# A spectral-mixing and gated MLP kernel: the sequence DFT in a three-fold split, with the odd half turned on ScalarE and GpSimd

## The chip, the cores and the metric

One core of a Trainium2 chip runs the whole kernel. The metric is the device time of the core in microseconds (us). A profile is one execution; "span" is its length, about 2 us below the timed value.

Engine names: PE is TensorE's matmul, PEld its weight load, DVE VectorE, ACT ScalarE, POOL GpSimd, SP SyncE. A fp32 matmul is two records in the trace. A "step" is one turn of the main loop; there are 376. A "record pitch" is the time from one PE record's start to the next.

## The reference

```python
def _attn_ref(x):                    # x: (8, 3008, 256) float32
    X = np.fft.fft(x, axis=1)        # over the sequence
    X = np.fft.fft(X, axis=2)        # over the channels
    return X.real.astype(np.float32)

def _moe_ref(x, w_in, w_out):        # (24064, 256), (256, 2048), (2048, 256)
    h = x @ w_in
    g = h * np.cos(h)
    return (g @ w_out).astype(np.float32)
# reference: the second of the first, with x reshaped to (24064, 256)
```

## The kernel before

The channel DFT is folded into `w_in` once (eight pairs of 512-column matmuls, giving `Wc` and `Ws`). The sequence DFT of a batch gives rings `Rr` and `Ir`, from which the main loop takes 256 columns a tile. Each step makes h on PE, its gate on ACT and DVE, four sums on POOL, and the second matmul with sums of w_out blocks (`WT`). The DFT of the next batch is spread over the loop: POOL folds rows `n` and `SEQ-n`, then PE multiplies folded rows by cosine and sine tables.

```python
# six row groups per batch of 128 (some partly used); even half and odd half
NH = (190, 189); NE = 377; NO = 376
def dft_parts(ri, kodd, par):
    mats = MC[ri, kodd]; nh = NH[kodd]
    if not par:                                   # four matmuls of 189/190 columns
        for t, m in enumerate((C0, Y, C2, Y)):
            yield m, t // 2 * nh, mats[:, t * nh : (t + 1) * nh]
        return
    c = 4 * nh
    if kodd: parts = ((D1, 0, NO), (X1, 0, NO), (M1, 0, NO))     # 3 x 376 columns
    else:    parts = ((6, 0, NK), (M1, NK, NE - NK), (X1, 0, NE))
    ...
# start: CC and half of w_in are loaded first, then batch 0's rows, then the rest
load_w1(0); L_first = load_x(0)
for g in gathers(0): gather_x(0, L_first, g)
...
# ... (cut)
def sum_weights(i):                               # WT by four POOL sums a pair of blocks
    gtt(W[2], b12, b22, ALU.add); gtt(W[1], b11, W[2], ALU.subtract)
    gtt(W[0], b12, b11, ALU.subtract); gtt(W[3], W[1], b21, ALU.add)
# batch 0's folds on DVE before the loop; those of later batches on POOL, spread over 36 steps
```

Of the kernel before, what the change touches and what calls it, by code (L numbers as in the profile page):

```python
# [26 lines left out]
NE = 377  # L27
NO = 376
NK = 189
NH = (190, 189)  # L30
MW = (4 * NH[0] + 2 * NE, 4 * NH[1] + 3 * NO)
C0, D1, C2, Y, M1, X1 = range(6)
# [4 lines left out]
def _row_of(m):  # L37

    p = np.arange(128)
    return (4 * p, 247 - 2 * p, 4 * p + 2, 504 + 2 * p, 505 + 2 * p, 249 + 2 * p)[m]  # L40


def _dft_consts():

    every = np.ones(128, bool)
    first, last = np.arange(128) % 2 == 0, np.arange(128) % 2 == 1
    used = {C0: 126, D1: 124, C2: 126, Y: 125, M1: 124, X1: 128}
    parts = []
    for kodd in range(2):
        if kodd:  # L50
            half = np.arange(NH[1])
            odd = [(m, every, np.arange(NO)) for m in (D1, X1, M1)]
        else:
            half = np.concatenate([np.arange(0, NH[0], 2), np.arange(1, NH[0], 2)])
            two = [np.arange(q, NE, 2) for q in range(2)]
            odd = [(D1, every, k) for k in two] + [(X1, every, np.concatenate(two))]
        even = [(C0, every, half), (Y, first, half), (C2, every, half), (Y, last, half)]
        for ri in range(2):
            fn = np.cos if ri == 0 else np.sin
            for m, keep, kk in even + odd:  # L60
                s = _row_of(m)
                k = 2 * kk + kodd
                v = fn(2.0 * np.pi * ((s[:, None] * k[None, :]) % SEQ) / SEQ)
                v[used[m] :] = 0.0
                v[s == 0] *= 0.5
                v[s == RUN] *= 0.5 if ri == kodd else 0.0
                v[~keep] = 0.0
                parts.append(v)
    return np.concatenate(parts, axis=1).astype(np.float32)
# [15 lines left out]
def _pick_consts():  # L85

    m = np.zeros((128, 56), np.float32)
    m[np.arange(128), np.arange(128) % 32] = 1.0
    q = np.arange(32)
    c = 32 + q % 16 // 2  # L90
    m[q, c] = 1.0
    m[q, c + 8] = np.where(q // 16 == q % 2, 1.0, -1.0)
    m[q, c + 16] = -1.0
    return m


def _row_consts():

    cols = [_row_of(D1), HALF + _row_of(D1)]
    for base in (HALF, SEQ):  # L100
        cols += [base - _row_of(m) for m in (C2, M1, X1)]
    cols += [SEQ - _row_of(m) for m in (C0, D1)]
    return np.clip(np.stack(cols, axis=1), 0, SEQ - 1).astype(np.uint32)
# [3 lines left out]
def kernel(  # L107
# [13 lines left out]
    MC_dr = nc.inline_tensor(_dft_consts(), name="dft_mats")  # L121
    CC_dr = nc.inline_tensor(_chan_consts(), name="chan_mats")
    PK_dr = nc.inline_tensor(_pick_consts(), name="pick_mats")
    IX_dr = nc.inline_tensor(_row_consts(), name="row_table")
# [15 lines left out]
    def xrows(b, row, step, n, rows=6):  # L140

        return bass.AP(
            tensor=xt,
            offset=x.offset + (b * SEQ + row) * ND,
            ap=[[step * ND, n], [1, rows * ND]],
        )
# [3 lines left out]
    ix = cpool.tile([128, 10], U32, tag="ix")  # L150
    nc.sync.dma_start(out=ix, in_=IX_dr.ap())

    def gather_x(b, L, g):

        j, part, n = g
        pin(
            nc.gpsimd.indirect_dma_start(
                out=L[j][:, part[0] * ND : part[1] * ND],
                out_offset=None,
                in_=xflat,  # L160
                in_offset=bass.IndirectOffsetOnAxis(ap=ix[:, n : n + 1], axis=0),
                element_offset=b * SEQ * ND,
            )
        )

    def spin(**kw):
        pin(nc.sync.dma_start(**kw))

    def gathers(b):

        yield 0, (1, 2), 0
        yield 3, (1, 2), 1
        for j, n in ((2, 2), (1, 5)):
            if j == 2 or b < NB - 1:
                yield j, (3, 6), n
            else:
                yield j, (3, 4), n
                yield j, (5, 6), 8
                yield j, (4, 5), 9
            yield j, (1, 3), n + 1  # L180
            yield j, (0, 1), n + 2

    def load_x(b):
        L = [
            spool.tile([128, 6 * ND], FP, tag=f"xl{j}", bufs=1, name=f"xl{j}")
            for j in range(4)
        ]
        for j, row in ((0, 0), (3, HALF)):
            spin(
                out=L[j].rearrange("p (m d) -> p m d", d=ND)[:, C0 : C2 + 1 : 2],  # L190
                in_=bass.AP(
                    tensor=xt,
                    offset=x.offset + (b * SEQ + row) * ND,
                    ap=[[4 * ND, 128], [2 * ND, 2], [1, ND]],
                ),
            )
            spin(out=L[j][:, Y * ND : X1 * ND], in_=xrows(b, row + 504, 2, 128, 2))
            spin(out=L[j][:, X1 * ND :], in_=xrows(b, row + 249, 2, 128, 1))
        return L

    def load_d(b, L, j):
        if b < NB - 1 or j == 2:
            row = SEQ if j == 1 else HALF
            spin(out=L[j][:, 4 * ND : 5 * ND], in_=xrows(b, row - 247, 2, 128, 1))



    CC = cpool.tile([128, 512], FP, tag="CC")
    spin(out=CC, in_=CC_dr.ap())
    w1 = {}  # L210

    def load_w1(half):
        for h in range(2):
            if h == 0:
                t = spool.tile([128, GW], FP, tag="G", bufs=3, name="w1")[:, 0:1024]
            else:
                t = spool.tile([128, 1024], FP, tag="ot", bufs=2, name="w1")
            w1[h, half] = t
            spin(
                out=w1[h, half],  # L220
                in_=moe_w_in[h * 128 : (h + 1) * 128, half * 1024 : (half + 1) * 1024],
            )

    load_w1(0)
    L_first = load_x(0)
    for g in gathers(0):
        gather_x(0, L_first, g)
    load_d(0, L_first, 2)
    load_w1(1)
    load_d(0, L_first, 1)  # L230

    def w1_cols(h, c0, c1):
        half = c0 // 1024
        return w1[h, half][:, c0 - half * 1024 : c1 - half * 1024]

    MC = {}
    w2 = cpool.tile([128, NF * ND], FP, tag="w2")
    for kodd in range(2):
        for ri in range(2):
            m = cpool.tile(  # L240
                [128, MW[kodd]], FP, tag=f"MC{ri}{kodd}", name=f"MC{ri}{kodd}"
            )
            c = kodd * 2 * MW[0] + ri * MW[kodd]
            spin(out=m, in_=MC_dr.ap()[:, c : c + MW[kodd]])
            MC[ri, kodd] = m
        if kodd == 0:
            spin(
                out=w2.rearrange("p (q c) -> p q c", c=ND),
                in_=moe_w_out.rearrange("(q p) c -> p q c", p=128),
            )  # L250
# [14 lines left out]
    pick = cpool.tile([128, 56], FP, tag="pick")  # L265
    nc.gpsimd.memset(R4, 0.0)
    nc.gpsimd.memset(Rx4, 0.0)
    spin(out=pick, in_=PK_dr.ap())
# [3 lines left out]
    PF = [cpool.tile([128, 128], FP, tag=f"pf{i}", name=f"pf{i}") for i in range(2)]  # L272
    pin(nc.gpsimd.memset(PF[1], 0.0))
    r4_dr = dpool.tile([1, NB], FP, tag="r4", name="r4")

# [23 lines left out]
    def fold_mms(q, part, tag):  # L299

        ps = bank(tag)
        for h in range(2):
# [3 lines left out]
                w1_cols(h, q * 512, (q + 1) * 512),  # L306
# [15 lines left out]
    def fold_cos(q, tag="H"):  # L322
# [4 lines left out]
    w2v = w2.rearrange("p (q c) -> p q c", c=ND)  # L327
    WT = [
        cpool.tile([128, 8, 128], FP, tag=f"WT{i}", name=f"WT{i}") for i in range(4)
    ]  # L330

    def sum_weights(i):
        b11, b12 = w2v[:, 2 * i, 0:128], w2v[:, 2 * i, 128:256]
        b21, b22 = w2v[:, 2 * i + 1, 0:128], w2v[:, 2 * i + 1, 128:256]
        W = [t[:, i] for t in WT]
        gtt(W[2], b12, b22, ALU.add)
        gtt(W[1], b11, W[2], ALU.subtract)
        gtt(W[0], b12, b11, ALU.subtract)
        gtt(W[3], W[1], b21, ALU.add)


    OC = slice(0, 6 * 127)

    def fold_x(L, eng, pieces):

        ops = {}

        def tt(o, a, b, f):
            pin(eng.tensor_tensor(out=o, in0=a, in1=b, op=f))

        def op(key, o, a, b, f):
            n = o.shape[1]
            cuts = [n * i // pieces for i in range(pieces + 1)]
            for i in range(pieces):
                c = slice(cuts[i], cuts[i + 1])
                ops[key, i] = lambda c=c: tt(o[:, c], a[:, c], b[:, c], f)

        E, O = [], []
        for j in range(4):
            e = spool.tile([128, 6 * 128], FP, tag=f"e{j}", bufs=1, name=f"e{j}")  # L360
# [4 lines left out]
            if j in (1, 2):  # L365
                src = src[:, ::-1]
# [65 lines left out]
    def dft_parts(ri, kodd, par):  # L432
# [12 lines left out]
        for m, o, n in parts:  # L445
            yield m, o, mats[:, c : c + n]
            c += n
# [840 lines left out]
```

## Time and profile before

1941.83 us, median of 3 runs (1940.52 to 1942.15). Where it goes, from the trace, by stretches of main-loop steps. "PE work" is the sum of each PE record's pitch as it is at full clock (215.6 ns for 256 columns; other widths at the pitches measured in the quiet loop); "lost" is the time taken minus that.

| stretch (kernel before) | took us | PE work us | lost us |
|---|---|---|---|
| start to first main matmul | 36.3 | | |
| steps 0 to 23 | 125.7 | 120.2 | 5.6 |
| steps 24 to 374 | 1759.7 | 1749.8 | 9.9 |

The page of the kernel before, its engine list and its chain of work that ended last:

```profile
PE 1921.9 (99%) x8878; PEld 1657.6 (85%) x8878; DVE 1426.7 (74%) x2387; ACT 1478.6 (76%) x2854; POOL 1412.0 (73%) x1926
...
PE 95%; DVE 2%; ACT 1%; issue 1%; DMA 1%; POOL 0%; SPq 0%; DVEq 0%; POOLq 0%
```

PE is the limit: it is busy for 99% of the span and 95% of the last chain is PE. POOL has 27% to spare. The groups of PE matmuls by shape, kernel before (name, shapes, count, busy us, mean ns, idle before):

```profile
L284 PE MATMUL pB<-G,WT 128*128 128x256 f32 x752 | 224.0, 379 | 1.0 <-POOL G L293 1.0
...
L284 PE MATMUL H<-MC,e 128*128 128x376 f32 x42 | 14.4, 479 | 0.0
...
L284 PE MATMUL H<-MC,e 128*128 128x190 f32 x56 | 10.2, 324 | 0.0
```

The DFT (`MC`) matmuls are 189 to 377 columns wide; PE waits for POOL's sums (`pB <- POOL`) only 1.0 us in all. The waits, kernel before (us in total, times, longest us):

```profile
PE H L284 <- DMA w<-in_moe_w_in_dram: 3.1, 2, 1.9
...
PEld pB L284 <- POOL G L293: 1.9, 3, 1.0
```

### The profile page before, as it was taken

What the parts mean: (1) busy time and instruction counts of PE and PEld (TensorE: products, weight loads), DVE (VectorE), ACT (ScalarE), POOL (GpSimd) and SP (SyncE); (2) the same over time, 40 slices, a digit from 0 to 9 for tenths busy, and PEclk for the clock granted to TensorE, in tenths of its full rate; (3) what the DMA queues carried; (4) which work ended last, traced back from release to release, by engine and by line L of the source; (5) the groups of instructions that cost most, each with busy time, mean ns of one, the idle gap of its engine ahead of it and who ended that gap; (6) DMA issues with size and microseconds to landing.
All of it is one profiled execution on the core that took longest, in us unless ns stands there. A gap on an engine that the chain in (4) does not pass through costs nothing.

```text
span 1939.9 us, 28429 instructions
## 1 busy us (share of the span) xinstructions
PE 1921.9 (99%) x8878; PEld 1657.6 (85%) x8878; DVE 1426.7 (74%) x2387; ACT 1478.6 (76%) x2854; POOL 1412.0 (73%) x1926
## 2 busy tenths in 40 slices
PE   8999999999999999999999999999999999999998
PEld 4888888888888888888888888888888888888887
DVE  5687777777777767777777777777767777677777
ACT  3777778877788777877778877787778777777786
POOL 6878768877687767877678776778768886555654
PEclk9999999999999999999999999999999999999999
DMA  9611210102101031110310103011030110000101
GB/s 274 35 29 17 61 47 20 18 14 71 33 20 18 11 78 31 18 20 9 87 27 13 22 7 94 13 21 26 7 84 15 24 27 7 17 12 12 21 10 25
DMA packets 258994, 67.59 MB, mean 35 GB/s; under 512 B 239970, under 2 KB 250858, under 8 KB 258842
## 3 DMA queue, kind: packets, MB, share of 16 engines
q1 hardware_dynamic: 251994, 50.81, 14.0%
q0 software_dynamic: 4672, 14.69, 2.6%
q8 instruction: 71, 1.16, 0.3%
q14 instruction: 81, 0.66, 0.1%
q10 hardware_dynamic: 2176, 0.26, 0.1%
HBM read 40.98 MB, written 24.69 MB: 34 GB/s over the span
## 4 chain that ended last, share of the span: by engine, by line
PE 95%; DVE 2%; ACT 1%; issue 1%; DMA 1%; POOL 0%; SPq 0%; DVEq 0%; POOLq 0%
PE H L284 38%; PE pC L284 17%; PE pD L284 16%; PE pB L284 16%; PE pA L284 8%; DMA w<-in_moe_w_in_dram 1%; DVE G L787 1%; ACT G L296 1%; DVE G L290 0%; ACT E L296 0%; DVE M L290 0%; DVE v L290 0%; DVE ab L290 0%; DVE ot L900 0%; DVE u L290 0%
## 5 line engine op out<-in xcount | busy, mean ns | idle before, releaser
L293 POOL TENSOR_TENSOR G<-G 128x256 f32<-128x256 f32 x1500 | 1076.6, 728 | 491.8 <-DVE G L787 426.7
L787 DVE SCALAR_TENSOR_TENSOR G<-H,G 128x512 f32<-128x512 f32 x376 | 259.2, 689 | 256.7 <-ACT G L296 256.4
L290 DVE TENSOR_TENSOR G<-H,G 128x512 f32<-128x512 f32 x376 | 260.0, 692 | 220.5 <-ACT G L296 217.5
L296 ACT ACTIVATE E<-H 128x512 f32<-128x512 f32 x376 | 224.4, 597 | 216.9 <-PE H L284 213.3
L284 PE MATMUL pC<-G,WT 128*128 128x256 f32 x1504 | 387.3, 379 | 2.1 <-DVE u L290 1.8
L284 PE MATMUL H<-Rr,Wc 128*128 128x256 f32 x1504 | 387.2, 380 | 0.7 <-ACT H L296 0.3
L284 PE MATMUL H<-Ir,Ws 127*128 127x256 f32 x1504 | 386.7, 378 | 0.7 <-ACT E L296 0.7
L296 ACT ACTIVATE H<-Rb,wex 128x256 f32<-128x256 f32 x752 | 360.6, 480 | 22.4 <-DVE G L787 8.1
L296 ACT ACTIVATE G<-H 128x512 int32<-128x512 f32 x376 | 224.5, 597 | 181.8 <-DVE G L290 180.6
L284 PEld LDWEIGHTS H<-Rr,Wc 128*128 128x128 f32 x1504 | 283.5, 190 | 48.5 <-ACT H L296 2.6
L284 PEld LDWEIGHTS pC<-G,WT 128*128 128x128 f32 x1504 | 283.7, 189 | 45.9 <-PE H L284 5.0
L284 PEld LDWEIGHTS H<-Ir,Ws 127*128 127x128 f32 x1504 | 284.7, 189 | 41.9 <-ACT E L296 1.4
L296 ACT ACTIVATE G<-G,halfpi 128x512 f32<-128x512 f32 x376 | 269.4, 717 | 0.6 <-DVE G L290 0.6
L290 DVE TENSOR_TENSOR M<-G,M 128x512 f32<-128x512 f32 x376 | 257.7, 685 | 0.0
L290 DVE TENSOR_TENSOR G<-E,H 128x512 f32<-128x512 f32 x376 | 255.5, 679 | 0.1
L787 DVE SCALAR_TENSOR_TENSOR G<-G,M 128x512 f32<-128x512 f32 x376 | 254.6, 677 | 0.6 <-ACT M L296 0.5
L296 ACT ACTIVATE M<-M,halfpi 128x512 f32<-128x512 f32 x376 | 246.1, 654 | 0.4 <-DVE M L290 0.3
L284 PE MATMUL pB<-G,WT 128*128 128x256 f32 x752 | 224.0, 379 | 1.0 <-POOL G L293 1.0
L296 ACT ACTIVATE M<-G 128x512 int32<-128x512 f32 x376 | 224.4, 597 | 0.0
L284 PE MATMUL pA<-G,w 128*128 128x256 f32 x752 | 223.8, 379 | 0.3 <-DVE G L787 0.3
L284 PE MATMUL pD<-G,WT 128*128 128x256 f32 x752 | 223.8, 379 | 0.0
L284 PE MATMUL pD<-G,w 128*128 128x256 f32 x752 | 223.7, 379 | 0.0
(147 smaller groups left out, 1886.6 us busy)
## 6 DMA issues: line engine op xcount, KB each, us to landing
out_dram<-ot SPq DMA_DIRECT2D x496, 32.0 KB
xl<-in_x_dram SPq DMA_DIRECT2D x32, 256.0 KB
out_dram<-ot SPq DMA_DIRECT2D x256, 2.0 KB
xl<-in_x_dram SPq DMA_DIRECT2D x31, 128.0 KB
Rb<-r SPq DMA_DIRECT2D x10, 376.0 KB
w<-in_moe_w_in_dram SPq DMA_DIRECT2D x4, 512.0 KB
w<-in_moe_w_out_dram SPq DMA_DIRECT2D x1, 2048.0 KB
MC<-dft_mats SPq DMA_DIRECT2D x2, 942.0 KB
```

The source lines that it names most:

```text
L284: nc.tensor.matmul(out_, lhsT=lhsT, rhs=rhs, start=start, stop=stop, skip_group_check=True)
L290: pin(nc.vector.tensor_tensor(out=o, in0=a, in1=b, op=op))
L293: pin(nc.gpsimd.tensor_tensor(out=o, in0=a, in1=b, op=op))
L296: pin(nc.scalar.activation(out=o, in_=i, func=func, **kw))
L787: nc.vector.scalar_tensor_tensor(out=o, in0=h, scalar=TWO_PI, in1=c, op0=ALU.mult, op1=ALU.mult)
```

## The change

Intent: use the factor 3 hidden in the row symmetry so that the DFT streams fewer columns through PE (even half 2 x 565 instead of 760 + 754, odd half 2 x 378 instead of 756 + 1128). The rows now lie in 8 slots of 96. The price is a "turning" of the odd half: scaled copies on ACT and sums on POOL. Some folds are done by DMAs that accumulate into SBUF. In the opening the rows are loaded ahead of the weights. For batch 0 the turning is split: the sine half on DVE, scalings included, the cosine half on POOL.

```diff
-C0, D1, C2, Y, M1, X1 = range(6)
+NP = 96; NS = 8; NA = 95; ORDER = (0, 3, 2, 1)
 ...
+    for j in ORDER: load_x(0, j)                # rows first
+    for g in gathers(0, ORDER): gather_x(*g)
     spin(out=CC, in_=CC_dr.ap())
     load_w1(0)
-    L_first = load_x(0) ...
+    load_mats(0); load_w1(1); load_mats(1); load_w1(2); load_w2(0, 4) ...
 ...
+        if kodd:                                # four matmuls of 94/95 columns
+            parts = ((0, p[0], ev, m[:, 0:95]), (0, p[1], od, m[:, 95:189]),
+                     (0, q[0], ev2, m[:, 189:284]), (0, q[1], od2, m[:, 284:378]))
+        else:                                   # two of 95, two of 188
+            parts = ((0, par, ..., m[:, 0:95]), (0, 4 + par, ..., m[:, 95:189]),
+                     (1, par, odd, m[:, 189:377]), (1, 3 - par, odd, m[:, 377:565]))
 ...
+    def add_by_dma(V, o, a, n):
+        pin(nc.gpsimd.dma_start(out=V[o][0:NP, 0:n], in_=V[a][0:NP, 0:n], accum_op=ADD))
+    def add_block(k, r, c):                     # WT partly by accumulating DMA
+        pin(nc.gpsimd.dma_start(out=WT[k][:, 2:8], in_=wout[r][...], accum_op=ALU.add))
 ...
+    p = pool_all(0, FOLD["R1"])                             # batch 0: cosine half on POOL
+    p = pool_all(p, flat(twist(VE[3], 0, VZ[0])))
+    n = dve_all(1, flat(twist(VO[2], 1, VZ[1])))            # sine half on DVE
 ...
+        for ri, V in ((0, VE[3]), (1, VO[2])):              # batches 1 to 7: ACT and POOL
+            p = pool_twist(max(p, done[ri] + 2), twist(V, ri, VZ[ri]))
```

## The prediction

> **What bounds the kernel now.** TensorE. The page's engine list has PE busy 99% of the span (DVE 74%, ACT 76%, POOL 73%), and the chain that ended last is 95% PE. Start-to-start in the timeline, each 256-column fp32 matmul is two records of 215.6 ns; a step is 22 of them, 4.74 us, and 376 steps are about 1784 us. The rest: opening (first main matmul at 36.3 us), the DFT, extras, a 7 us tail; waits are few.
>
> **What the change removes.** DFT columns on TensorE. Before, per batch and per cos/sin: even half 760+754 columns, odd half 756+1128; at the trace's pitches (160 ns a record for 190 columns, 316 for 376) that is 11.5 us a batch. After: even 2x565, odd 2x378. Counted by columns, a batch saves 11.5 − 6.3 = 5.2 us. But many of the new matmuls have only 94 or 95 columns (80 ns of streaming a record), each with its own 128-column weight load. The 20 "pick" records before, with 8 or 16 columns, show what such a load costs when nothing hides it: 108 to 118 ns start to start at full clock. [...] So I cost short records at 117, the 188-column ones at 158: even 2.20 us, odd 1.87, a batch 8.1 us. Saved: 3.3 us a batch, **23 us for the seven batches in the loop**, all on the critical path.
>
> **What it adds and moves.** The turning goes to POOL (sums), ACT (scaled copies) and accumulating DMAs. POOL's main sums take 3.02 us a step; the folds now take about 1 us of every step. The new plan allows 1.75 us, 4.77 in such steps, over the 4.74 period. Per batch I add up about 61 us against 43 on POOL, so it reaches about 82% of the span. The sum that feeds pB has 0.7 us of slack in the worst tenth of steps; I expect some waits of pB on POOL: **+7 us** (guess 0 to 20). ACT gains 24 scaled copies a batch (some 7 us of 230); it should not bind, nor DVE.
>
> **Opening.** Rows come before weights, and the DFT constants shrink from 3.5 to 1.2 MB, so rows should be complete at about 15.5 us, not 21.8. But folding w_in moves behind them, and eight 512-column fold matmuls plus one early DFT move into the first steps. First main matmul at about 32 us (−4), then about +4 us of extra PE work and perhaps a wait for the last w_in quarter: **net 0 ± 6**. One-channel transform: +1.
>
> Sum: 1942 − 23 + 0 + 1 = **1920 us** without new stalls, 1927 with all 7 us. The opening may give more than I count, so I stay at **1920, range 1902 to 1938**. Chances: faster by over 2% 0.12, within 2% 0.85, slower 0.03.
>
> **What would show each step.** Right: DFT records of 95 columns at about 117 ns and 188 at 158; PE still over 98%; the main step still 4.74 us; POOL 80 to 84%; first main matmul at 30 to 34 us. Wrong: 95-column records at 80 ns (then 10 us faster); pB waits on POOL of over 15 us in the waits view; a first main matmul under 28 or over 36 us.
>
> **What would make it wrong.** POOL pacing whole stretches (over 1938); weight loads hidden better, or an opening 10 us shorter (under 1903).

The 117 ns rest on the pick records (in the trace 14 of their 19 pitches are 108 to 118 ns, one is 120, the first four are 233 to 256). The 80 ns for 94 or 95 columns are an estimate, half of the 160 ns that 190 columns took.

## More of the kernel before

"Steps 0 to 3" runs from the start of step 0 to the start of step 4. The "granted clock" is the share of full TensorE speed that the clock record shows: 1, or 0.5 ("half clock").

Before the loop PE hardly waits for w_in. The windows of steps 0 to 3, 4 to 7, 8 to 15 and 16 to 23, kernel before (stretch, length, busy us of PE, PEld, DVE, ACT, POOL with counts, granted clock, DMA share, GB/s):

```profile
36.30:58.90 22.60, 21.56 (x92) 16.88 (x93) 18.10 (x37) 14.65 (x29) 20.63 (x37) 1.00 1.11 74
58.90:78.00 19.10, 19.10 (x91) 16.76 (x90) 12.70 (x20) 14.97 (x30) 18.24 (x32) 1.00 1.13 86
78.00:123.50 45.50, 44.40 (x226) 36.42 (x225) 33.42 (x58) 32.05 (x63) 31.03 (x45) 1.00 0.12 21
123.50:162.00 38.50, 38.18 (x177) 33.12 (x176) 29.70 (x48) 30.87 (x59) 33.31 (x45) 1.00 0.13 25
```

## The result

1938.38 us median of 4 runs (1937.32 to 1938.97) against 1941.51 (1940.52 to 1942.15) of the kernel before in the same rounds. The ratio is 0.9984, 95% interval 0.9966 to 1.0001: the same within 2%, and hardly told apart from no gain. Ratios are the mean time of one kernel's runs over that of the other's of the same rounds, so not quite the ratio of the medians quoted. It lies just above the predicted range of 1902 to 1938, and 18 us above the predicted figure.

| stretch | before: took, work, lost | after: took, work, lost | difference |
|---|---|---|---|
| to first main matmul | 36.3 | 36.9 | +0.6 |
| steps 0 to 3 | 22.6, 21.0, 1.6 | 31.0, 22.0, 9.1 | +8.4 |
| steps 4 to 7 | 19.0, 19.0, 0.0 | 22.4, 20.8, 1.7 | +3.4 |
| steps 8 to 15 | 45.5, 42.2, 3.3 | 50.7, 44.3, 6.4 | +5.2 |
| steps 16 to 23 | 38.6, 38.0, 0.7 | 40.2, 38.0, 2.3 | +1.6 |
| steps 24 to 374 | 1759.7, 1749.8, 9.9 | 1737.2, 1724.8, 12.5 | −22.5 |

So the loop gave what the prediction said (23 less a few stalls), and the first 24 steps took 18.6 us of it back: 5.0 of more PE work, which was predicted, and 13.9 of more loss (5.6 to 19.5), which was not (rounding apart). The experiments are about those 13.9. The page of the changed kernel:

```profile
PE 1899.4 (98%) x8951; PEld 1646.7 (85%) x8951; DVE 1450.9 (75%) x2366; ACT 1513.3 (78%) x2985; POOL 1525.5 (79%) x2054
...
PE 87%; ACT 5%; DVE 5%; issue 1%; POOL 1%; DMA 0%; DVEq 0%; POOLq 0%; ACTq 0%
```

PE's share of the last chain falls from 95% to 87%: the chain now leaves PE in the opening. The groups of PE matmuls by shape, changed kernel:

```profile
L292 PE MATMUL pB<-G,WT 128*128 128x256 f32 x752 | 225.4, 381 | 4.7 <-POOL G L301 4.7
...
L292 PE MATMUL H<-MC,z 94*128 94x188 f32 x56 | 11.7, 330 | 0.0
...
L292 PE MATMUL H<-MC,e 95*128 95x95 f32 x46 | 8.5, 265 | 0.0
```

Means of records overlap their neighbours; start to start, the 94- and 95-column records come mostly every 109 to 112 ns and the 188-column ones every 158 to 162 (the first record of each DFT visit 86, the first 188-column one 190). PE's waits for POOL grow to 4.7 us in all, every one of them between 36 and 175 us. The waits, changed kernel:

```profile
PE H L292 <- DMA w<-in_moe_w_in_dram: 12.0, 1, 12.0
...
PEld pB L292 <- POOL G L301: 10.0, 18, 2.5
```

With the rows first, PE waits 12.0 us for w_in, and its first real work begins at 18.3 us. The windows of the same four stretches, changed kernel:

```profile
36.90:67.90 31.00, 26.54 (x92) 18.67 (x93) 18.38 (x29) 17.41 (x33) 23.44 (x29) 0.89 1.80 70
67.90:90.30 22.40, 21.12 (x105) 18.24 (x104) 18.36 (x28) 15.34 (x30) 20.07 (x29) 1.00 0.19 51
90.30:141.00 50.70, 46.43 (x242) 38.83 (x241) 42.02 (x77) 33.15 (x68) 35.99 (x50) 1.00 0.19 46
141.00:181.00 40.00, 39.08 (x176) 32.69 (x176) 35.41 (x52) 31.04 (x60) 36.66 (x47) 1.00 0.40 84
```

Two things stand out: the granted clock is 0.89 in the first window (0.5 from 38.3 to 45.1 us in the clock record), and DVE is busy for 82 to 89% of the later three. What DVE does there, from its timeline in the changed kernel (start us, length us, what):

```profile
66.10 0.68 DVE L298 TENSOR_TENSOR G<-E,H 128x512 f32<-128x512 f32 x1
66.70 2.94 DVE L373 TENSOR_TENSOR z<-o,RC 96x254 f32<-96x254 f32 x1
69.56 0.68 DVE L298 TENSOR_TENSOR G<-H,G 128x512 f32<-128x512 f32 x1
```

and PE's and POOL's timelines at that place:

```profile
66.56 0.76 POOL L301 TENSOR_TENSOR G<-G 128x256 f32<-128x256 f32 x1
67.25 1.43 POOL L301 TENSOR_TENSOR WT<-WT,w 128x256 f32<-128x256 f32 x2
68.61 3.28 POOL L301 TENSOR_TENSOR G<-G 128x256 f32<-128x256 f32 x4
...
71.08 0.70 PE L292 MATMUL pB<-G,WT 128*128 128x256 f32 x2 [1.28 <-POOL G L301]
```

A turning operation of 254 elements (0.42 us is what 256 elements with two SBUF inputs take here with POOL idle) took 2.94 us while POOL ran sums back to back; the loop's own DVE operations on either side, which read one operand from PSUM, kept 0.68 us (0.64 to 0.69 in all 1504 of such operations). PE then stood 1.28 us. Between 35 and 216 us there are 40 DVE operations with two SBUF inputs that lie mostly beside POOL's sums (five in the kernel before), and they look like this: 254 elements, with POOL busy, 0.55 to 2.94 us (median 0.83, ten of them); 508 elements 0.67 to 1.85 us (median 1.0, fourteen) against 0.68 with POOL idle. Each of the ten of 254 elements ended 0.28 to 0.29 us after a POOL sum did.

The prediction did not ask what these operations would run beside.

### The profile page after: what moved, and what is told of

It is laid out like the page before. It is cut to its first block, busy times and chain, and to the rows that moved or that the text cites. A ratio compares the mean times of both kernels' runs of the same rounds, so it can differ in the third digit from the quotient of the medians.

```text
span 1936.3 us, 28827 instructions
## 1 busy us (share of the span) xinstructions
PE 1899.4 (98%) x8951; PEld 1646.7 (85%) x8951; DVE 1450.9 (75%) x2366; ACT 1513.3 (78%) x2985; POOL 1525.5 (79%) x2054
## 4 chain that ended last, share of the span: by engine, by line
PE 87%; ACT 5%; DVE 5%; issue 1%; POOL 1%; DMA 0%; DVEq 0%; POOLq 0%; ACTq 0%
PE H L292 34%; PE pC L292 15%; PE pD L292 15%; PE pB L292 15%; PE pA L292 8%; ACT G L304 1%; DVE G L829 1%; DVE G L298 1%; ACT M L304 1%; ACT E L304 1%; ACT z L304 1%; POOL G L301 1%; ACT H L304 0%; DVE v L298 0%; DVE M L298 0%
## 5 line engine op out<-in xcount | busy, mean ns | idle before, releaser
L292 PE MATMUL pB<-G,w 128*128 128x256 f32 x752 | 223.7, 379 | 0.0
```

The costliest lines, as they stand in the source:

```text
L292: nc.tensor.matmul(out_, lhsT=lhsT, rhs=rhs, start=start, stop=stop, skip_group_check=True)
```

## The experiments

Theory A: the 13.9 us are several separate things in the opening: half clock, DVE held beside POOL, and POOL's own turning work. Rival B: they are one thing, the opening's order of loads (rows before weights). Rival C, for the loop: weight loads of the short records, or POOL, give back part of the gain. (The expectations use names of their own: "theory C" is the half clock, "theory P" the pacing by DVE and POOL.)

The losses by stretch come from one profile of each kernel and are counted from the first main matmul. In steps 4 to 23 they repeat well: 10.4 us also in e1, e3 and e6, whose edits do not reach these steps. The first main matmul does not repeat as well: kernels with the same opening have it at 36.9 (changed kernel), 37.0 (e2), 35.8 (e4) and 38.2 us (e5), and the kernel before at 36.3 and 34.5 (e10). Shifts of it below about 2 us are not told apart.

### e1_warm: eight and four one-row matmuls in the gaps

```diff
     fold_cos(1)
+    warm(8)                 # mm(bank, zero[1 row, 128], zero[1 row -> 512]) x8
     fold_now("o1 O0 I0")
 ...
+        (0.87, lambda: warm(4)),
         (0.88, lambda: first_I.early("pA", "M")),
```

> Eight dummy matmuls before the first main step and four after its first matmuls, in time in which TensorE waits anyway. Theory C (the half clock of 6.8 us in the opening is what costs): no stretch of clock 0.5 after 30 us, step 4 starts at about 59 us instead of 62.6, and the 3.5 us stay to the end: 1935 us. Theory P (VectorE and GpSimd pace the first 24 steps): step 4 starts earlier, but by step 24 under 1 us is left: 1938 us.

Correct; 1943.41 us (1939.24 to 1949.04), ratio 1.0019 (1.0002 to 1.0035); why some of its runs were that long is not explained. (The 62.6 us of the expectation is where the fourth step starts, step 3 as numbered here.) The half clock stayed (38.9 to 45.7 us), though PE had no gap above 0.25 us from 31.3 to 52. Its timeline:

```profile
35.49 1.91 PE L292 MATMUL M<-zero 1*128 1x512 bf16 x8
37.33 1.13 PE L292 MATMUL H<-Rr,Wc 128*128 128x256 f32 x4
38.40 1.42 PE L292 MATMUL M<-zero 1*128 1x512 bf16 x4
39.75 1.17 PE L292 MATMUL pA<-MC,o 95*128 95x95 f32 x4
```

The four 95-column matmuls after them take 1.17 us instead of 0.58. These one-row bf16 matmuls of zeros fill PE in the trace but did not hold the clock. The experiment failed as a test of the clock's price; e6 repeats it.

### e2_memsets: DVE's two-input fold operations of the loop replaced (wrong result)

```diff
     def tto(eng, o, a, b, op):
+        if state.get("stand"):                  # set around DVE's folds of the loop
+            pin(nc.vector.memset(o, 0.0))
+            return
```

> Wrong result on purpose: the VectorE sums with two SBUF inputs in the main loop (turning of the first batch's imaginary part, one-channel folds, second batch's odd folds) are replaced by memsets of the same outputs, so VectorE is busy as long but reads nothing. Theory P (those sums are held up by GpSimd's work, and hold up the loop): TensorE's loss in steps 8 to 24 falls from 8.7 us to about 3, and the kernel takes about 1932 us. If VectorE merely has too much to do there: within 1.5 us of 1938. Theory C (clock): no change, 1938.

1933.18 us (1929.6 to 1934.71), ratio 0.9959 (0.9942 to 0.9976). The same stretches lost 1.4, 2.9 and 0.8 us in steps 4 to 7, 8 to 15 and 16 to 23: 5.1 instead of 10.4. The memsets write the same tiles in the same places, and the operation that took 2.94 us is now

```profile
63.08 0.27 DVE L374 MEMSET z<- 96x254 f32 x1
```

So 5.3 us of the 13.9 go with these sums. That is an upper figure for the holding: the memsets are shorter than sums that nothing holds (0.27 us against 0.42 for 254 elements, 0.48 against 0.68 for 508), so that DVE is not "busy as long", as the expectation has it, and part of the 5.3 may be the lighter load on DVE. e10 tests the holding itself. By luck this profile also had no half clock, and steps 0 to 3 lost 4.8 instead of 9.1; that part does not belong to this edit.

### e3_weights_first: rows behind CC and half of w_in, as before

```diff
-    for j in ORDER: load_x(0, j)
-    for g in gathers(0, ORDER): gather_x(*g)
     spin(out=CC, in_=CC_dr.ap())
     load_w1(0)
-    load_mats(0)
     load_w1(1)
+    for j in ORDER: load_x(0, j)
+    for g in gathers(0, ORDER): gather_x(*g)
+    load_mats(0)
```

> Undoes one part of the change: the channel matrix and two quarters of the input weights are loaded before the rows, as before the change. If rows first helps: first main matmul 3 to 5 us later than 36.9, kernel about 1941. If rows first starves the weights and that is what the opening pays: first main matmul the same or earlier, kernel about 1935.

Correct; 1938.93 us, ratio 0.9990 (0.9973 to 1.0007). The first main matmul comes 3.1 us later (40.0), but the half clock now lies before it (20.4 to 37.5), steps 0 to 3 lose 5.0 instead of 9.1, and step 4 begins at 67.0 us against 67.9. Rival B falls: the order of loads moves the loss and leaves the sum. The loss in steps 4 to 23 is the same 10.4 us.

### e4_half_loads: 64 weight columns in the loop's DFT (wrong result)

```diff
             n, parts = dft_parts(self.ri, self.kodd, par)
+            m = 128 if start else 64
             for src, slot, o, rhs in parts:
-                mm(ps[:, o], self.stat(src, slot, n), rhs, start, False)
+                mm(ps[0:m, o], self.stat(src, slot, n)[:, 0:m], rhs, start, False)
```

> Wrong result on purpose: the DFT matmuls of the loop load 64 weight columns instead of 128, with the same moving columns. If the weight load sets the pace of the 94 and 95 column records (as predicted): their pitch falls from 111 to about 81 ns, the 188 column ones stay at 158, and the kernel takes about 10 us less, 1928. If something else sets a floor: pitch 111 and 1938.

1947.34 us, ratio 1.0034 (1.0017 to 1.005): slower than the kernel before by 0.3%, and some 9 us longer than the changed kernel where 10 shorter was expected. The 95-column records did come mostly every 83 ns instead of 111, so the load was what paced them, and PE work in steps 48 to 374 fell from 1605.7 to 1596.3 us; but loss there rose from 11.5 to 29.1. The PE timeline around one DFT visit, in the changed kernel and then in e4:

```profile
441.60 0.59 PE L292 MATMUL pD<-G,w 128*128 128x256 f32 x2
442.03 0.58 PE L292 MATMUL H<-MC,e 95*128 95x95 f32 x4
442.45 0.83 PE L292 MATMUL H<-MC,z 95*128 95x188 f32 x4
443.12 1.03 PE L292 MATMUL H<-Rr,Wc 128*128 128x256 f32 x4
443.98 0.59 PE L292 MATMUL pA<-G,w 128*128 128x256 f32 x2
```

```profile
442.19 0.59 PE L292 MATMUL pD<-G,w 128*128 128x256 f32 x2
442.71 0.54 PE L292 MATMUL H<-MC,e 95*64 95x95 f32 x4
443.10 0.80 PE L292 MATMUL H<-MC,z 95*64 95x188 f32 x4
443.83 1.13 PE L292 MATMUL H<-Rr,Wc 128*128 128x256 f32 x4
444.79 0.59 PE L292 MATMUL pA<-G,w 128*128 128x256 f32 x2
```

From the first line to the last it is 2.38 us there and 2.60 here: the pitches around each change of weight width grow (0.52 instead of 0.43 us into the visit, 0.96 instead of 0.86 behind it). Why they grow where the number of weight columns changes is not shown.

### e5_pool_skip: POOL's turning of batch 0 left out (wrong result)

```diff
-    p = pool_all(0, FOLD["R1"])
+    p = pool_all(0, no(FOLD["R1"]))             # same plan, no instructions
 ...
-    p = pool_all(p, flat(twist(VE[3], 0, VZ[0])))
+    p = pool_all(p, no(flat(twist(VE[3], 0, VZ[0]))))
```

> Wrong result on purpose: GpSimd's turning of the first batch's real part (one difference, six scalings, eight sums, some 11 us of GpSimd in steps 0 to 8) is left out, its place in the schedule is kept. Theory P (GpSimd paces the first 8 steps): the waits of pB for GpSimd in the opening (4.7 us) are nearly gone, step 8 starts 4 us or more earlier than 90.3, and VectorE's two-input sums beside it get shorter; kernel about 1933. If GpSimd is not what paces: under 1 us earlier, 1938.

1936.1 us (1933.59 to 1936.5), ratio 0.9967 (0.9951 to 0.9984). Steps 0 to 3 lose 6.2 instead of 9.1, with the half clock still there (39.8 to 46.6); the rest is all but unchanged (10.1 in steps 4 to 23). By this count POOL's extra work costs 2.9 us there. The expectation was met by half: step 8 began at 88.5 us, 1.9 earlier and not 4 (the first main matmul came 1.3 us later in this profile), and PE's waits of pB for POOL fell from 4.7 to 2.4 us.

### e6_real_warm: three real 128-row matmuls instead of e1's twelve one-row ones

```diff
+    def warm2(n):
+        w = bank("M")
+        for _ in range(n):
+            mm(w, CC[:, 0:128], CC, True)
     ...
     fold_cos(1)
+    warm2(2)
 ...
+        (0.87, lambda: warm2(1)),
```

> The warm run showed a half clock in spite of dummy matmuls of one row of zeros; here three dummy matmuls of 128 rows of real data stand in two of TensorE's waits instead. Theory C: no stretch of clock 0.5 from 38 to 45 us in most runs, steps 0 to 4 lose about 5 us instead of 9.1, kernel about 1934. If dummies do not keep the clock: 1938 or slower.

Correct; 1935.29 us (1934.86 to 1937.34), ratio 0.9966 (0.995 to 0.9983). No half clock after 30.9 us, and the mean granted clock was 0.998 to 0.999 in its runs, against 0.996 to 0.997 in the changed kernel's. Steps 0 to 3 lose 5.0 instead of 9.1. Not all of these 4.1 us are the clock: the dummies' own 0.9 us inside these steps count as PE work, and they fill time in which PE stood before (0.74 us at 38.0). In time taken the steps fell from 31.0 to 27.8 us, by 3.2; and 6.8 us at half clock can cost about 3.4 at most, an estimate from e1, where records at half clock took twice as long (1.17 us instead of 0.58). The same place as shown for e1:

```profile
37.51 1.88 PE L292 MATMUL M<-CC 128*128 128x512 f32 x4
39.24 1.13 PE L292 MATMUL H<-Rr,Wc 128*128 128x256 f32 x4
40.20 1.02 PE L292 MATMUL M<-CC 128*128 128x512 f32 x2
41.06 0.58 PE L292 MATMUL pA<-MC,o 95*128 95x95 f32 x4
```

The matmuls behind the dummies run at full pace: 0.58 us for the four of 95 columns, which took 1.14 at half clock in the changed kernel. Whether the rows, the data or the type of the dummies made the difference to e1 was not separated, and what lowers the clock is not shown. Stretches at half clock lasted 3.4 us (e8, e17), 6.8 (changed kernel, e1, e12) or 17.1 (e3). In e8 and e17 below it fell 4.5 us into a wait of PE of 5.05 us and 2.9 us into one of 3.24; but in the changed kernel PE's longest gap in the 3.4 us before was 1.57 us, so a gap of that length was not needed there. Where they fall differs between profiles with the same opening (38.3 us in the changed kernel, 39.8 in e5, none in e2).

### e7_replanned: batch 0's scalings to ACT, the one-channel transform earlier

```diff
-    p = pool_all(p, flat(twist(VE[3], 0, VZ[0])))
+    p = pool_twist(p, twist(VE[3], 0, VZ[0]))          # scalings by ACT, sums by POOL
 ...
-    n = dve_all(1, flat(twist(VO[2], 1, VZ[1])))
+    n_i = dve_twist(1, twist(VO[2], 1, VZ[1]))         # scalings by ACT, sums by DVE
 ...                                                   # batch 1's gathers planned later (cut)
-    s = bank_step(max(8, extra[-1] + 2))
+    s = bank_step(5)                                   # one-channel transform
```

> Right result: in the opening the scalings of the first batch's turning go to ScalarE copies (as in all later batches), VectorE and GpSimd keep the sums; the one-channel transform is planned three steps earlier. Theory P: steps 4 to 16 lose some 4 us less, kernel about 1934. If it is not VectorE and GpSimd: within 1.5 us of 1938.

Correct; 1934.29 us (1932.86 to 1938.9), ratio 0.9965 (0.9949 to 0.9982). Steps 8 to 23 lose 4.7 instead of 8.7, but steps 4 to 7 3.9 instead of 1.7. The edit moves the scalings to ACT and also moves the one-channel transform and batch 1's gathers, so this run does not say which of them the gain belongs to; the half clock was still there (39.3 to 46.2).

### e8_relieved: e7 with the start reordered and one real dummy

```diff
-    turn_last(0)                                       # moved behind add_O(2, 3), an accumulating DMA
 ...
-    fold_cos(1)
-    fold_now("o1 O0 I0")
-    add_O(2, 0)
+    fold_now("o1 O0")
     first_R.plus()                                     # the sum that makes Rr
+    fold_now("I0")
+    add_O(2, 0)
 ...
+        (-1.0, lambda: fold_cos(1)),
+        (0.87, lambda: warm2(1)),
```

> e7 and also a reordered start: the accumulating DMA is issued before the column turns, the even sums are written before the odd ones, the fold of the second quarter's cosines comes after the first step's opening copy, and one real dummy matmul. First main matmul about 1.5 us earlier than 36.9, the rest as in e7 with the half clock present or not: about 1932.

Correct; 1936.26 us (1932.54 to 1938.12), ratio 0.9969 (0.9953 to 0.9986): no better than e7. The first main matmul comes at 35.7 us, but behind it PE meets

```profile
52.91 2.07 PE L292 MATMUL H<-Ir,Ws 127*128 127x256 f32 x4 [5.05 <-ACT E L304]
```

In its timeline ACT stands for 2.87 us at a copy of negated weights whose accumulating DMA has not landed (it lands at 49.8 us), and the copy that PE needs comes behind it, at 52.27; the granted clock then falls to half (52.4 to 55.8).

### e9_ledger: e2, e5 and e6 together (wrong result)

> Result wrong on purpose. Three earlier edits of the changed kernel at once: DVE's two-input fold operations of the loop replaced by memsets, POOL's batch-0 turning left out, three real 128-row dummy matmuls in the opening to hold the clock. If these three causes are separate and add up (ledger theory): steps 0 to 24 lose 7 to 9 us (19.5 in the changed kernel, 5.6 before), DVE's other work unchanged, median about 1926 (1938.4 minus 4 to 5 for the clock, 5 for the held operations, 2 to 3 for POOL). If they overlap (rival: one common delay of which each edit removes the same part), steps 0 to 24 still lose 13 or more and the median is about 1932.

1929.99 us (1928.03 to 1933.66), ratio 0.9945 (0.993 to 0.996). Steps 0 to 23 lose 4.1 + 1.2 + 2.8 + 0.6 = 8.7 us, as theory A said, against 19.5 in the changed kernel. The median was 4 us above the figure expected: the dummies are 0.8 us of work and the first main matmul came 1.5 us later. So 10.8 of the 13.9 us go with these three causes. In time taken steps 0 to 23 are 9.7 us shorter (134.7 against 144.4): as in e6, 0.9 us of dummies are counted as work. In steps 0 to 3 they overlap: removed one at a time, clock and turning give 4.1 + 2.9, together with the memsets 5.0. The other 3.1 us are not removed by any run. Most of them lie in steps 0 to 3 (4.1 against 1.6 before), and there e9's trace has one wait of PE, for the E that ACT copies (PE and ACT):

```profile
52.88 1.13 PE L292 MATMUL H<-Ir,Ws 127*128 127x256 f32 x4 [3.41 <-ACT E L304]
...
50.31 0.84 ACT L304 ACTIVATE WT<-WT 128x768 f32<-128x768 f32 x1 [1.81 <-DMA WT<-in_moe_w_out_dram]
```

ACT had stood at a copy of weights whose accumulating DMA had not landed, as in e8. The kernel before makes `WT` by POOL sums alone and has 0.7 us of this wait in the same steps. That this DMA costs the rest is read from the trace, not shown by a run.

### e10_control: one added DVE operation a step in the kernel before

```diff
+    pad = cpool.tile([128, 188], FP, tag="pad", name="pad")
+    for i in range(60, 300):
+        if i < 180:
+            at(i * T + 1.12, lambda: vtt(pad, CC[:, 0:188], CC[:, 256:444], ALU.add))
+        else:
+            at(i * T + 1.12, lambda: pin(nc.vector.memset(pad, 0.0)))
```

> The kernel before, result right, with one added DVE operation per step: in steps 60 to 180 a sum of two SBUF constants (188 elements), in steps 180 to 300 a memset of the same 188 elements at the same place. Theory (a DVE operation with two SBUF inputs is held while POOL's sums run): the added sum lasts 335 ns where POOL is idle and 0.6 to 1.1 us where it is busy, median above 0.6; the memset always under 0.3 us. If DVE has the room, both stretches keep 4.74 us a step; otherwise the first takes some tens of us more than the second. Rival (the added operations of the changed kernel are long for another reason, such as SBUF traffic of the DMAs or of the opening): in this quiet stretch both last their nominal time and no step grows.

Correct; 1947.14 us (2 runs), ratio 1.0032 (1.0014 to 1.005). Steps 60 to 179 took 605.9 us (601.0 before, so +4.9), steps 180 to 299 with the memset 599.7 (599.6 before). The two added groups, from the view of their tile (duration ns min/median/max):

```profile
L290 DVE TENSOR_TENSOR pad<-CC x120: 308/347/1149, 346.7 to 946.9; 128x188 f32<-128x188 f32 x120
L1230 DVE MEMSET pad<- x120: 215/215/215, 952.0 to 1548.0; 128x188 f32 x120
```

The expected median above 0.6 us was wrong: most of these operations met the end of a POOL sum or none at all and kept 0.35 us. But 24 of 120 took over 0.45 us, and record by record they show a pattern. Of the 25 that began with over 0.2 us of a POOL sum still to run, 23 ended 206 to 213 ns after that sum did, whatever was left of it (0.39 to 0.94 us). Two examples, DVE and then POOL:

```profile
435.59 0.70 DVE L290 TENSOR_TENSOR pad<-CC 128x188 f32<-128x188 f32 x1
...
440.75 0.35 DVE L290 TENSOR_TENSOR pad<-CC 128x188 f32<-128x188 f32 x1
```

```profile
435.08 1.00 POOL L349 TENSOR_TENSOR e<-e,e 128x384 f32<-128x384 f32 x1
...
440.82 1.14 POOL L349 TENSOR_TENSOR e<-e,e 128x384 f32<-128x384 f32 x1
```

At 435.59 the DVE operation comes second and is long (0.70); at 440.75 it comes first, keeps 0.35 us, and POOL's fold behind it takes 1.14 instead of 1.00 us (median 1.13 of 42 such). So the DVE operations that came second ended behind a POOL sum (23 of 25), and the POOL folds that came second took 0.13 us longer; by what mechanism is not shown. The 2.94 us operation fits this pattern, here shown apart from the opening: it too ended 0.29 us behind a POOL sum, the fourth in a row.

### e11_combined and e12_combined_late

e11 is e7 with e6's three dummies. e12 is e11 with

```diff
-        (T + 0.2, lambda: less_block(1)),
-        (T + 0.25, lambda: add_block(1, 0, 0)),
+        (1.65 * T, lambda: less_block(1)),
+        (1.65 * T + 0.05, lambda: add_block(1, 0, 0)),
```

> Result right: the changed kernel with batch 0's scalings on ScalarE and the one-channel transform planned earlier (as e7) and three real dummy matmuls in the opening (as e6). If the two gains add up: no half clock after 31 us, steps 0 to 24 lose 10 to 12 us, median 1929.5 to 1931.5, faster than both kernels by about 0.4 to 0.6 per cent. If they overlap: 1933 to 1935, like either alone.

> Result right: as e11, and ScalarE's copy of the negated weights for the second WT block, with the accumulating DMA behind it, moved 0.45 of a step later, so that ScalarE's in-order stream does not stand at it. If the wait seen in e8 (PE waiting 5 us for ScalarE's E) costs something here too: 1 to 2 us faster than e11. If in e11's order the DMA has landed in time: same as e11 within 1 us.

e11 is correct: 1932.16 us (5 runs, 1931.17 to 1936.16), ratio 0.9961 (0.9947 to 0.9975); steps 0 to 23 lose 12.4. It lies a little above the additive figure (1929.5 to 1931.5), so the gains add for the most part. e12 is correct: 1934.81 us, ratio 0.9966 (0.995 to 0.9981). No gain. Its profile had the half clock at 58.0 to 64.8 us, which adds to the loss in steps 0 to 3; PE's waits there show an exchange: for ACT's E 1.7 us instead of 3.2, but a new one of 3.3 for POOL.

### e13_late_wout and e14 to e16: is w_out's traffic what makes the rows late?

The prediction had the rows complete at 15.5 us; the last gather lands at 20.4 and the last row fold on DVE begins at 22.2. The gathers take 9.0 us from issue to landing in the opening, 3.1 in the loop. e13 is the changed kernel with

```diff
     def load_w2(a, z):
-        spin(out=w2[...], in_=...)              # SP's queue
+        pin(nc.gpsimd.dma_start(out=w2[...], in_=...))   # POOL's, behind the gathers
-    spin(out=WT[2][:, 2:8], in_=...)
+    pin(nc.gpsimd.dma_start(out=WT[2][:, 2:8], in_=...))
```

> Result right: the changed kernel, with the three loads of w_out (2.4 MB) issued by POOL behind its gathers instead of by the sync queue beside them. If the weights' traffic is what makes the rows late: the gathers land 4 to 7 us after issue instead of 9.0, DVE's last row fold starts at 17 to 20 us instead of 22.2, and the first main matmul comes at 33 to 35. If the gathers' own issue pace holds them (1.22 us each, last at 12.3 us): they still land near 9 us after issue, last fold at 21 to 22.5, first main matmul within 0.7 us of 36.9. Median: 1935 to 1938.

Correct; 1943.8 us, ratio 1.0011 (0.9994 to 1.0028). The gathers still land 9.2 us after issue and the last row fold begins at 22.5: w_out's traffic is not the cause. What the edit did was to put 2.4 MB ahead of the accumulating DMA (381 KB) in POOL's queue, which then took 12.2 us from issue to landing instead of 7.7 (medians of two; 4.9 in the loop):

```profile
37.92 1.21 DVE L375 TENSOR_TENSOR o<-o,o 96x1016 f32<-96x1016 f32 x1 [5.79 <-DMA o<-o]
```

DVE waits 5.8 us for the DMA, the sum that makes `Rr` stands behind it, and the first main matmul comes at 41.1 us. In the changed kernel the same wait is 0.75 us.

e14 is e11 with that edit, e15 is e8 with it and with e12's shift, e16 is e14 with `first_R.plus()` ahead of the last odd folds.

> Result right: e11 (scalings on ScalarE, one-channel transform earlier, three real dummies) with the w_out loads behind the gathers as in e13. If earlier rows reach the first main matmul: at 34 to 35.5 us instead of 37.4 and median 1929 to 1931. If DVE's order or the w_in folds hold it: within 0.7 us of 37.4 and the median of e11, 1932.

> Result right: e8's order of the start (sum that makes Rr ahead of the last fold, one w_in fold behind the first main matmul, one real dummy) with ScalarE's weight copy 0.45 step later, and the w_out loads behind the gathers. If all three delays of the start are separate: first main matmul at 31 to 34 us (35.7 in e8), no PE wait of over 3 us for ScalarE's E, median 1927 to 1930. If the clock falls to half again, 1930 to 1934.

> Result right: e14 with the sum that makes Rr put ahead of the last two odd folds on DVE (only this reordered). Expected 0.5 to 1.5 us earlier first main matmul than e14 and a median up to 1.5 us lower; the same if the copy of the last w_in fold on ScalarE holds it, as the waits of the changed kernel say (PE waiting 1.57 us for ScalarE's H there).

All correct: 1941.69, 1940.21 and 1940.25 us (ratios 0.9994, 0.9995, 0.9990), first main matmul at 42.0, 38.4 and 41.2 us. e14 and e16 are longer than e11 and e18, the same kernels without the edit; e15 is not told apart from e17. The gathers' own issue pace (one every 1.22 us, the last issued by 12.3) does not suffice to make the rows late: with the 3.1 us to landing that they take in the loop, the last would land at about 15.4, an estimate from these two figures and close to the prediction's 15.5. The rest is the 9.0 us to landing; what makes it so long, the other weights beside the rows or something else, stays open.

### e17_start_late_copy and e18_combined_order

e17 is e8 with e12's shift; e18 is e11 with `first_R.plus()` ahead of the last odd folds.

> Result right: e8 with only ScalarE's second weight copy and the DMA behind it moved 0.45 step later. If ScalarE's in-order stream stood at that copy because the accumulating DMA before it had not landed: the longest PE wait for ScalarE's E falls from 5.9 us to under 3, no half clock near 52 us, steps 0 to 4 lose 3 to 5 us less than in e8, median 1931 to 1933. If the wait came from elsewhere: within 1 us of e8.

> Result right: e11 with the sum that makes Rr ahead of the last odd folds on DVE (e16 without the held-back loads). Expected first main matmul 0 to 1.5 us earlier than e11's 37.4, median 1931 to 1932.5; if the fold order does not matter, the same as e11.

e17 is correct: 1939.32 us (1933.86 to 1941.46), ratio 0.9989 (0.9972 to 1.0005). The wait of e8 did go, as expected, from 5.05 to 1.71 us; but 16 records on, PE meets the next:

```profile
49.97 1.13 PE L292 MATMUL H<-Ir,Ws 127*128 127x256 f32 x4 [1.71 <-ACT E L304]
...
57.88 1.22 PE L292 MATMUL pB<-G,WT 128*128 128x256 f32 x2 [3.24 <-POOL G L301]
```

and the half clock returns (57.5 to 60.9). Steps 0 to 3 lose 8.4 instead of 9.5: the expected 3 to 5 us did not come. Its run at a mean clock of 0.998 took 1933.9 us, the three at 0.995 to 0.997 took 1939.2 to 1941.5.

e18 is correct: 1933.45 us (1932.31 to 1935.23), ratio 0.9953 (0.9936 to 0.997), not told apart from e11; its first main matmul (37.9) came no earlier.

e11 and e18 beat both kernels: they are 0.4 to 0.5% faster than the kernel before. Against the changed kernel (0.9984) they ran in other rounds; their medians are 5 to 6 us lower while the kernel before stood at 1941 to 1942 in all of them.

A variant in which POOL's sums stand in place of the accumulating DMAs of later batches deadlocked in its plan and was not run, so the price of those DMAs in the loop is not measured.

## Why the prediction was wrong

- **What bounds the kernel: right.** PE stays at 98%, the main step at 22 records of 215.6 ns.
- **The loop's gain, 23 us less stalls: right.** Steps 24 to 374 took 22.5 us less: 25.0 of PE work, since short records came mostly every 109 to 112 ns instead of the estimated 117, less 2.6 of more loss. e4 shows that the load, not the streaming, paces these records: with 64 weight columns they came every 83 ns instead of 111.
- **POOL stalls, +7 (0 to 20): too high, in the loop.** POOL reached 79% (predicted about 82, with 80 to 84 named as the sign), and all of the loss in steps 24 to 374 grew by 2.6 us. PE's own waits of pB for POOL are 4.7 us against 1.0, and all lie before 175 us, 2.1 of them in steps 0 to 3.
- **The rows at 15.5 us: wrong.** The last gather lands at 20.4 and the last row fold begins at 22.2; a gather took 9.0 us to land here, against 3.1 in the loop. e13 shows that w_out's traffic is not the reason; what is stays open.
- **First main matmul at about 32 (−4): wrong.** It came at 36.9 (+0.6). The prediction's own sign, "over 36", says so.
- **The step that failed: "net 0 ± 6" for the opening.** With +0.6 to the first main matmul and +18.6 in steps 0 to 23 it was +19.2. The +5 of PE work was there. The sum had a term for a late w_in quarter and none for new stalls there. What was missing is 13.9 us of loss: e9 takes 10.8 of it away by removing three things. Singly measured they are half clock (4.1 by the count of losses, 3.2 in time taken, e6), DVE's two-input sums beside POOL (up to 5.3, e2) and POOL's turning of batch 0 (2.9, e5), with some overlap; 3.1 is not settled.
- **"It should not bind, nor DVE": wrong in the opening.** The prediction added busy time to DVE and did not ask which of the added operations read two SBUF tensors. Before, five did so beside POOL, after, 40; the main loop's read one operand from PSUM.

## What to carry to other kernels

Before giving VectorE an elementwise operation with two SBUF inputs, look at what GpSimd does at that time. Here 23 of 25 such operations of 188 elements that began with over 0.2 us of a GpSimd sum still to run ended 206 to 213 ns after that sum (e10), and one of 254 elements lasted 2.94 us beside four sums in a row, where 256 elements take 0.42 with GpSimd idle. Operations with a PSUM operand kept 0.64 to 0.69 us, and the scaled copies on ScalarE 0.38 to 0.39, in every batch. A gain in a loop's steady state and a loss in its first steps have to be summed from separate stretches, since shares of the whole span show neither. Removing one wait in the opening showed the next one (e8: 5.05 us, e17: 3.24), as did moving loads (e13: 5.8), and in e8 and e17 3.4 us of half clock came on top, from the last 0.4 to 0.5 us of the wait on.
